# Second layer, second product of the last two batches: seven block products for eight, kept apart over the groups of weights

## The chip, the cores and the metric

The kernel runs on one core of a Trainium2 chip. The metric is the time of one execution in device microseconds, as a median over runs. In the profiles the engines are PE (TensorE), DVE (VectorE), ACT (ScalarE), POOL (GpSimd) and SP, on whose queue every DMA of this kernel is issued.

## The reference

Attention over four batches of 448 tokens, then two layers over 1792 tokens with a model width of 768 and an inner width of 2048. Only the last layer is touched:

```python
def _moe2_ref(x, w_in, w_out) -> np.ndarray:
    h = x @ w_in
    r = np.maximum(h, 0.0)
    g = r * r
    return (g @ w_out).astype(np.float32)
```

All data are float32. The kernel splits each float32 operand of a layer's products into an upper part in TensorE's own float32 form and a lower part (the rest), and sums three matmuls for each product: upper with upper, upper with lower, lower with upper.

## The kernel before, in words

`layer2` handles the four batches in two halves of two batches (896 tokens). In each half it goes through eight groups of weights; a group is two blocks of 128 inner features. For each group:

- **First product** (`seven`, line 1064). Four 448-token by 128-feature blocks of h come from seven block products instead of eight. Each is nine matmuls of 448 columns (line 1075). The sums of the products run on DVE (`plus`, line 1090: `g<-t`), and each finished block goes through `finish`: relu and square on ACT (lines 1338, 1344), then `split` into `gh` and `gl` (lines 523, 525: casts; line 532: subtraction, on DVE or POOL). In the trace the seven products are told by their operands: `pv<-raw,w` and `pv<-xb,w` are the two halves of p1, `t<-yb,w` are p6 and p7, `t<-xb,w` is p5, `t<-xb,v` is p4 and `t<-part,w` is p3.
- **Second product** (line 1367). Seven chunks of 128 tokens by two halves of 384 output columns, each the sum of six matmuls of 384 columns in a PSUM buffer `s`, of which there are four. That is 84 matmuls a group. One `acc` step per buffer adds it to the sum in SBUF, `gg` (line 1394, DVE; in the first group a copy on ACT, line 1388).
- After the last group each chunk of `gg` is stored (line 1408).

The weights of the first product are computed once, in the first half, and kept in DRAM as split parts (`sw`, `sz`, `sv`, `sa`); those of the second product too (`su`). In the second half all are loaded back (line 927) into a ring `w` of five buffers and `v`. The words of the second product's weights, not yet split, also lie in DRAM as `kq`.

Nothing fixes the order of the two layers by hand. Each operation is a `step` with the engines that may do it and their costs; a planner (`Plan.forward`, `Plan.backward`) takes the step that can start first by its own cost model, chooses between DVE, POOL and ACT, and issues everything in that order. A step that reads two SBUF tensors on DVE and any step on POOL exclude each other in the planner (the third entry of a cost). Attention has a written timetable, and isn't touched.

## Time and profile before

| | us |
|---|---|
| median of 3 runs | 1192.38 |
| the runs | 1186.67, 1192.38, 1195.06 |
| the profiled execution | 1184.83 |
| its span on the core | 1183.0 |

The profiled execution lies 7.55 us under the median, and 1.83 us of it are outside the span. All times of rows below belong to that one execution. A row of instructions gives their number, the mean duration of one, and the idle time of the engine just ahead of them with what ended it. Durations of DVE overlap where instructions follow each other without a gap: the busy time of a run of several tells how far their starts lie apart.

### The profile page before, as it was taken

The page shows a single profiled execution, that of the slowest core. Times are in us where ns is not written, and L with a number is a line of the kernel's source. Part 1 is how long each engine was busy: PE and PEld are TensorE (multiplying, and loading weights), DVE is VectorE, ACT ScalarE, POOL GpSimd, SP SyncE. Part 2 cuts the span into 40 slices and gives each one's busy share as a digit, 9 for nine tenths or more (in the row PEclk, how much of TensorE's full clock was granted, in tenths as well). Part 3 has the DMA queues.
Part 4 walks back from the last instruction along what each step waited for, and adds up shares of the span by engine and source line. Part 5 has one row for each costly group of instructions (what it writes and reads, how often), then busy time and mean ns, then how long its engine had stood idle before and what let it go on. Part 6 is the DMA issues. An engine that isn't in the chain of part 4 may idle for free.

```text
span 1183.0 us, 18930 instructions
## 1 busy us (share of the span) xinstructions
PE 1156.8 (98%) x6888; PEld 1035.5 (88%) x6888; DVE 921.4 (78%) x1612; ACT 551.3 (47%) x1154; POOL 239.4 (20%) x445
## 2 busy tenths in 40 slices
PE   5999999999999999999999999999999999999998
PEld 3777777778899999999999999899999989999997
DVE  7999999987999999965689898789887843555544
ACT  5999999874443334422325262544333423111111
POOL 3566676531000010000001020011131300000000
PEclk9999999999999999999999999999999999999999
DMA  7455557639998888732247649888768694444443
GB/s 171 86 78 90 90 91 102 96 63 204 298 285 271 251 276 289 228 110 63 82 172 228 240 153 359 268 298 310 262 245 293 191 322 154 147 147 147 149 170 122
DMA packets 136700, 224.86 MB, mean 190 GB/s; under 512 B 31392, under 2 KB 102048, under 8 KB 136608
## 3 DMA queue, kind: packets, MB, share of 16 engines
q1 hardware_dynamic: 136608, 223.67, 63.0%
q8 instruction: 54, 0.88, 0.4%
q14 instruction: 38, 0.31, 0.1%
HBM read 149.32 MB, written 74.31 MB: 189 GB/s over the span
## 4 chain that ended last, share of the span: by engine, by line
PE 91%; DVE 5%; DMA 3%; issue 1%; SPq 0%; ACT 0%; DVEq 0%; ACTq 0%
PE s L1164 19%; PE s L1367 18%; PE t L1075 18%; PE t L988 7%; PE t L712 7%; PE pv L1075 7%; PE pv L761 6%; PE s L685 6%; PE t L632 2%; DMA raw<-in_moe_w_in_dram 1%; DMA w<-sz 1%; DVE w L532 1%; DMA qk<-in_k_dram 0%; DVE g L1090 0%; DVE W L903 0%
## 5 line engine op out<-in xcount | busy, mean ns | idle before, releaser
L1164 PE MATMUL s<-gg,w 128*128 128x448 f32 x1152 | 238.8, 365 | 0.8 <-DVE gg L532 0.7
L1164 PEld LDWEIGHTS s<-gg,w 128*128 128x128 f32 x1152 | 216.2, 188 | 18.8 <-DVE gg L532 1.4
L1367 PE MATMUL s<-w,gh 128*128 128x384 f32 x896 | 227.7, 334 | 0.7 <-DVE gg L1394 0.7
L1367 PEld LDWEIGHTS s<-w,gh 128*128 128x128 f32 x896 | 162.3, 188 | 2.2 <-DVE gg L1394 1.1
L1090 DVE TENSOR_TENSOR g<-t,g 128x448 f32<-128x448 f32 x144 | 87.3, 620 | 93.1 <-ACT g L511 53.9
L1394 DVE TENSOR_TENSOR gg<-s,gg 128x384 f32<-128x384 f32 x196 | 107.0, 554 | 57.0 <-PE s L1367 56.6
L1367 PE MATMUL s<-w,gl 128*128 128x384 f32 x448 | 150.0, 335 | 0.9 <-DVE gl L532 0.8
L703 ACT ACTIVATE E<-s,mx 112x448 f32<-112x448 f32 x192 | 122.1, 647 | 20.6 <-ACT xf L511 13.0
L988 PE MATMUL t<-xb,w 128*128 128x448 f32 x576 | 119.2, 366 | 0.7 <-ACT g L1000 0.7
L988 PEld LDWEIGHTS t<-xb,w 128*128 128x128 f32 x576 | 108.0, 188 | 10.2 <-ACT g L1000 1.0
L523 ACT CAST w<-W 128x768 fp32r<-128x768 f32 (+1 forms) x73 | 54.5, 750 | 125.4 <-PE s L1164 46.5
L532 DVE TENSOR_TENSOR w<-W,w 128x768 fp32r<-128x768 f32 (+1 forms) x121 | 107.3, 896 | 6.8 <-ACT w L523 5.9
L696 DVE TENSOR_REDUCE mx<-s 112x1 f32<-112x448 f32 x192 | 107.4, 610 | 6.1 <-PE s L685 5.4
L712 PEld LDWEIGHTS t<-ident,E 112*112 112x112 f32 x768 | 73.8, 134 | 32.0 <-issue 14.6
L712 PE MATMUL t<-ident,E 112*112 112x112 f32 x768 | 95.3, 267 | 0.8 <-DVE T L648 0.4
L1367 PEld LDWEIGHTS s<-w,gl 128*128 128x128 f32 x448 | 84.1, 188 | 1.9 <-DVE gl L532 1.9
L761 PE MATMUL pv<-PT,vv 112*64 112x224 f32 x768 | 83.1, 359 | 0.0
L1075 PE MATMUL t<-yb,w 128*128 128x448 f32 x360 | 80.2, 372 | 2.4 <-DMA w<-sz 2.4
L1075 PE MATMUL t<-xb,w 128*128 128x448 f32 x360 | 79.9, 367 | 0.0
L511 ACT COPY g<-pv 128x448 f32<-128x448 f32 x24 | 12.7, 531 | 140.1 <-PE pv L1075 130.6
L1075 PEld LDWEIGHTS t<-yb,w 128*128 128x128 f32 x360 | 68.5, 191 | 8.5 <-DMA w<-sz 2.7
L685 PE MATMUL s<-T 64*112 64x448 f32 x576 | 73.1, 384 | 2.6 <-ACT T L641 1.9
(119 smaller groups left out, 1803.7 us busy)
## 6 DMA issues: line engine op xcount, KB each, us to landing
raw<-in_moe_w_in_dram SPq DMA_DIRECT2D x25, 768.0 KB
raw<-in_moe_w_out_dram SPq DMA_DIRECT2D x24, 512.0 KB
su<-w SPq DMA_DIRECT2D x16, 768.0 KB
w<-su SPq DMA_DIRECT2D x16, 768.0 KB
xf<-y SPq DMA_DIRECT2D x48, 224.0 KB
raw<-in_moe_w_out_dram SPq DMA_DIRECT2D x10, 768.0 KB
ki<-W SPq DMA_DIRECT2D x16, 384.0 KB
ko<-W SPq DMA_DIRECT2D x24, 256.0 KB
```

The costliest lines, as they stand in the source:

```text
L532: kind, when, any_t(n, rate), lambda e: engine(e).tensor_tensor(o(), a(), h(), ALU.subtract),
L685: nc.tensor.matmul(pts[j].ap[:CP, :S], T.ap[r, 0, a, c * CP:(c + 1) * CP], T.ap[r, 1, b_], start=(k_ == 0), stop=(k_ == 2),)
L696: lambda e, pt=pt, mx=mx: nc.vector.tensor_reduce(mx.ap, pt.ap[:CP, :S], AX.X, ALU.max, negate=True),
L703: lambda e, j=j, c=c, pt=pt, mx=mx, E=E: nc.scalar.activation(E.ap[:, j], pt.ap[:CP, :S], AF.Exp, bias=mx.ap, accum_out=sums.ap[:, j, c:c ...
L712: nc.tensor.transpose(pe.ap[:CP, m * CP:(m + 1) * CP], E.ap[:, j, m * CP:(m + 1) * CP], ident.ap)
L761: nc.tensor.matmul(pv.ap[j * D:(j + 1) * D, c2 * CT * CP:(c2 + 1) * CT * CP], vr.ap[:, j * NCH + m, :], pt.ap[:, j * NCH + m].rearrange("p ...
L988: nc.tensor.matmul(pt.ap[:, :S], w_()[:, c, :], x[c // HC].ap[:, a, c % HC, :], start=(c == 0 and n == 0), stop=(c == NC6 - 1 and n == 2),)
L1075: nc.tensor.matmul(pt.ap[:, :S], w_()[:, c0 + c, :], view(b, a, c)(), start=(start and c == 0 and k == 0), stop=(c == HC - 1 and k == 2), ...
L1090: lambda e: nc.vector.tensor_tensor(o.ap, pt.ap[:, :S], a.ap, ALU.add),
L1164: nc.tensor.matmul(pt.ap[:, :S], w_()[:, f, :], gg.ap[:, k, a, f, :], start=(f == 0 and n == 0), stop=(f == HQ - 1 and n == 2),)
L1367: nc.tensor.matmul(pt.ap[:, :NH], g.ap[:, fi, tc_ * P:(tc_ + 1) * P], w_()[:, 0, nh * NH:(nh + 1) * NH], start=(n == 0), stop=(n == 5),)
L1394: lambda e, o=o, pt=pt: nc.vector.tensor_tensor(o(), pt.ap[:, :NH], o(), ALU.add),
```

## The change

For the second half alone (`SEVEN2 = (1,)`), and there for the first seven of the eight groups, the second product is made in blocks too. Of the 896 tokens, 384 of each batch are taken as the two token halves (`LEFT`, three chunks of 128 each, `NPAIR`); the remaining 128 tokens (64 of each batch) are one chunk that is done as before. The two blocks of inner features and the two halves of 384 output columns are the other halves. The seven products of a group are added over the groups without being joined: P3, P4, P5 and C11 into the four places of `gg`, U2 and P7 into six buffers of the ring `xf`. Before the last group, which is done as before, `join` forms the result with five additions for each of the three chunks.

What is added for each of the seven groups:

- two loads of 384 KB (`V<-kq`), four differences of 384 columns (`w_sum`) and two splits of 768 columns (`w_hi2`, `w_lo2`) for the weights;
- four sums of 384 columns (`h_sum`) and four splits (into `part` and a buffer of the ring `W`) for g; one of the plain splits shrinks from 448 to 64 columns;
- 23 additions to SBUF in place of 14.

In these groups `seven` makes p5 ahead of p4 (`fifth`). In the last group the order of the chunks alternates between the batches, and the stores name their rows accordingly.

```diff
+SEVEN2 = (1,)
-    def seven(x, w, at, finish):
+    def seven(x, w, at, finish, fifth=False):
...
+        if fifth:
+            p5 = psum("t")
+            product(p5, z, 0, "T1")
+            plus(c21, u3, p5)
+            finish(1, 1, c21)
+            plus(u2, u2, p5)
+            c21 = u3
         p4 = psum("t")
         product(p4, a22, 0, "T4")
...
+            later = products7(total, LEFT, NPAIR) if half in SEVEN2 else None
             for fg in range(NG):
+                sums = later is not None and fg < NG - 1
...
+                    c0 = LEFT if sums and (fi, bi) == (1, 0) else 0
...
+                    if sums:
+                        later.sums(fi, bi, whole, at)
+                seven(x, w, ("end", t), finish, sums)
+                if sums:
+                    later.weights(f0, f1, at)
+                    t = later.down(gh, gl, wo, fg, t, DOWN2)
+                    continue
+                if later is not None:
+                    later.join(("end", t - 7 * PROD))
...
+    class products7:
+        def __init__(self, total, left, npair):
+            self.part = sb([P, 2 * NC6 * S // 2], FR, "part", None, "yp")
+            self.block = sb([P, 2 * HC * S], FR, "xb")
+            self.word = [sb([P, UW], FR, "W") for _ in range(2)]
+            self.more = {(n, m): sb([P, S], F32, "xf") for m in range(npair) for n in ("U2", "P7")}
...
+        def sums(self, fi, bi, g, at):
+            if (fi, bi) == (0, 0):
+                less(A22, A21, A22, ALU.add)
+                put("S1", A22)
+                less(A22, A22, A11)
+                put("S2", A22)
+                less(A21, A11, A21)
+                put("S3", A21)
+            if (fi, bi) == (0, 1):
+                less(A12, A12, A22)
+                put("S4", A12)
+
+        def weights(self, f0, f1, at):
+            W0, W1 = (second_out(f, at, "V", "yp") for f in (f0, f1))
+            less(W1, 0, W1, 1, W1, 0)
+            less(W1, 1, W0, 1, W1, 1)
+            less(W0, 1, W0, 1, W1, 0)
+            less(W0, 0, W0, 0, W0, 1)
+            for n, W in (("13", W1), ("42", W0)):
+                (h, hk), (l, lk) = self.T[n]
+                split(("w_hi2", "w_lo2"), at, h, l, lambda W=W: W.ap, [W], [hk, lk], DM)
+
+        def down(self, gh, gl, wo, fg, t, DOWN2):
+            ops = {
+                1: (raw(1, 1), given(1, 0)), 2: (raw(0, 1), given(0, 0)), 3: (summed("S4"), given(0, 1)),
+                4: (raw(0, 0), made("42", 0)), 5: (summed("S1"), made("13", 0)), 6: (summed("S2"), made("42", 1)),
+                7: (summed("S3"), made("13", 1)),
+            }
+            for n in (4, 5, 7, 1, 6, 3):
+                for m in range(self.npair):
+                    pt = psum("s")
+                    product(n, m, pt, True, t)
+                    add_to(*into({1: "U2", 6: "U2"}.get(n, f"P{n}"), m), pt, fg == 0 and n != 6, ("end", t))
+                    if n == 1:
+                        product(2, m, pt, False, t)
+                        add_to(*into("C11", m), pt, fg == 0, ("end", t))
...
+        def join(self, at):
+            for m in range(self.npair):
+                for n, a in (("P3", "U2"), ("P3", "P5"), ("U2", "P7"), ("P5", "U2"), ("P4", "U2")):
```

Here `product` issues three matmuls of 384 columns, `raw` are `gh` and `gl`, `given` the loaded weights, `summed` the four sums of g and `made` the differences of the weights. The line of the new matmuls is 1544, that of the plain ones 1422, of the additions 1438; other lines of the parts above move by one.

How the planner lays the work out has changed as follows. **TensorE, a late group of the second half** (from the middle of its first product on). Before:

```order
L1075 MATMUL t<-yb,w 128x448 x18
L1075 MATMUL pv<-raw,w 128x448 x9
L1075 MATMUL t<-xb,v 128x448 x9
L1075 MATMUL pv<-xb,w 128x448 x9
L1075 MATMUL t<-xb,w 128x448 x9
L1075 MATMUL t<-part,w 128x448 x9
L1367 MATMUL s<-w,gh 128x384 x2
L1367 MATMUL s<-w,gl 128x384
```

Now, rows that repeat a triple left out:

```order
L1076 MATMUL t<-xb,w 128x448 x9
L1076 MATMUL pv<-xb,w 128x448 x9
L1076 MATMUL t<-xb,v 128x448 x9
L1076 MATMUL t<-part,w 128x448 x9
L1544 MATMUL s<-xb,gh 128x384
L1544 MATMUL s<-W,gh 128x384
L1544 MATMUL s<-xb,gl 128x384
...
L1076 MATMUL pv<-raw,w 128x448 x9
L1544 MATMUL s<-xb,part 128x384 x18
L1544 MATMUL s<-w,gh 128x384 x2
L1544 MATMUL s<-w,gl 128x384
```

The 84 plain matmuls in one piece have become 63 new ones and 12 plain ones, and p1 of the next group (`pv<-raw`) has moved up to stand 9 matmuls after p3; products 5 and 7 (`s<-xb,part`) stand behind it.

**VectorE, the same group.** Before, where the second product is summed:

```order
L1090 TENSOR_TENSOR g<-t,g 128x448 x3
L525 CAST gh<-g 128x448
L1394 TENSOR_TENSOR gg<-s,gg 128x384 x2
L532 TENSOR_TENSOR gl<-g,gh 128x448
L1394 TENSOR_TENSOR gg<-s,gg 128x384 x12
```

Now:

```order
L1438 TENSOR_TENSOR gg<-s,gg 128x384 x3
L533 TENSOR_TENSOR part<-g,part 128x384
L1091 TENSOR_TENSOR g<-t,g 128x448
L1438 TENSOR_TENSOR gg<-s,gg 128x384 x3
L1438 TENSOR_TENSOR xf<-s,xf 128x384 x7
L1438 TENSOR_TENSOR gg<-s,gg 128x384 x2
L533 TENSOR_TENSOR W<-g,part 128x384
L1438 TENSOR_TENSOR gg<-s,gg 128x384
L1438 TENSOR_TENSOR xf<-s,xf 128x384 x2
L533 TENSOR_TENSOR W<-V,xb 128x768
```

Between the additions there now stand subtractions for the split parts (`W<-g,part`, `W<-V,xb`), and 15 additions answer to one stretch of 45 matmuls.

**TensorE, the end of the first half**, where the second half's p1 and p6 begin among the last 84 plain matmuls. Before:

```order
L1075 MATMUL pv<-raw,w 128x448 x9
L1367 MATMUL s<-w,gh 128x384 x2
L1367 MATMUL s<-w,gl 128x384
L1367 MATMUL s<-w,gh 128x384 x2
L1367 MATMUL s<-w,gl 128x384
L1075 MATMUL t<-yb,w 128x448 x9
```

Now:

```order
L1076 MATMUL pv<-raw,w 128x448 x9
L1422 MATMUL s<-w,gh 128x384 x2
L1422 MATMUL s<-w,gl 128x384
...
L1422 MATMUL s<-w,gh 128x384 x2
L1422 MATMUL s<-w,gl 128x384
L1076 MATMUL t<-yb,w 128x448 x9
```

There are 24 plain matmuls between the two now (6 before).

## Rows read from the trace of the kernel before

**Rows 1.** First part of the page: busy time, share, number of instructions by engine.

```profile
PE 1156.8 (98%) x6888; PEld 1035.5 (88%) x6888; DVE 921.4 (78%) x1612; ACT 551.3 (47%) x1154; POOL 239.4 (20%) x445
```

**Rows 2.** All waits of TensorE: total us, times, longest.

```profile
PE t L632 <- POOL y L611: 11.4, 1, 11.4
PE t L1075 <- DMA w<-sz: 2.4, 1, 2.4
...
PE s L1367 <- DVE gg L1394: 0.7, 1, 0.7
```

**Rows 3.** Chain that ended last, in order of time: start, us, what.

```profile
1108.52 14.56 PE s L1367 x84
1123.08 3.71 PE t L1075 x18
...
1136.06 14.56 PE s L1367 x84
```

**Rows 4.** Stretches: busy time of each engine, granted clock, DMA share, GB/s.

```profile
460.00:500.00 40.00, 40.00 (x199) 37.09 (x198) 37.43 (x68) 19.16 (x36) 2.58 (x2) 1.00 0.71 229
680.00:720.00 40.00, 40.00 (x199) 37.03 (x198) 37.77 (x66) 23.12 (x41) 7.32 (x5) 1.00 0.61 193
937.05:970.66 33.61, 30.03 (x149) 27.42 (x148) 16.39 (x31) 8.50 (x16) 7.06 (x6) 0.95 0.91 309
950.75:953.00 2.25, 2.25 (x6) 2.04 (x7) 0.00 (x0) 0.00 (x0) 0.00 (x0) 0.50 1.02 399
1073.00:1073.50 0.50, 0.50 (x4) 0.46 (x3) 0.00 (x0) 0.00 (x0) 0.00 (x0) 1.00 0.04 12
1108.36:1135.90 27.54, 27.54 (x149) 26.39 (x148) 14.20 (x26) 5.47 (x11) 1.16 (x1) 1.00 0.47 158
```

**Rows 5.** Instructions by line, whole span: count, busy us, mean ns, idle before.

```profile
L1394 DVE TENSOR_TENSOR gg<-s,gg 128x384 f32<-128x384 f32 x196 | 107.0, 554 | 57.0 <-PE s L1367 56.6
L1090 DVE TENSOR_TENSOR g<-t,g 128x448 f32<-128x448 f32 x144 | 87.3, 620 | 93.1 <-ACT g L511 53.9 <-PE t L1075 35.9 <-issue 1.3
L897 DVE SCALAR_TENSOR_TENSOR V<-raw,V 128x768 int32<-128x768 int32 x19 | 18.1, 952 | 0.3
L1052 DVE TENSOR_TENSOR W<-W 128x384 f32<-128x384 f32 x26 | 15.1, 592 | 0.3
L525 DVE CAST gh<-g 128x448 fp32r<-128x448 f32 x35 | 14.1, 409 | 15.2 <-ACT g L1344 15.1
L1052 POOL TENSOR_TENSOR W<-W 128x384 f32<-128x384 f32 x6 | 7.2, 1197 | 37.4 <-DVE W L1033 33.7 <-DVE w L532 3.7
L532 POOL TENSOR_TENSOR w<-W,w 128x768 fp32r<-128x768 f32 (+1 forms) x7 | 11.9, 1707 | 56.9 <-ACT w L523 56.9
```

**Rows 6.** Timeline between the halves, of all engines: start, us, what [idle before].

```profile
930.74 5.37 POOL L1216 TENSOR_TENSOR xf<-xf 128x448 f32<-128x448 f32 x1 [14.11 <-DMA xf<-y]
938.92 0.64 SPq L927 DMA_DIRECT2D w<-sz  x1
940.60 1.15 POOL L532 TENSOR_TENSOR xb<-xf,xb 128x448 fp32r<-128x448 f32 x1 [0.68 <-ACT xb L523]
941.03 0.97 DVE L525 CAST gh<-g 128x448 fp32r<-128x448 f32 x1 [2.34 <-ACT g L1344]
941.92 1.47 DVE L1394 TENSOR_TENSOR gg<-s,gg 128x384 f32<-128x384 f32 x3
942.52 0.62 PE L1367 MATMUL s<-w,gh 128*128 128x384 f32 x2 [0.75 <-DVE gg L1394]
945.18 2.10 PE L1075 MATMUL pv<-raw,w 128*128 128x448 f32 x9 [0.31 <-DMA w<-sw]
950.75 3.50 PE L1075 MATMUL t<-yb,w 128*128 128x448 f32 x9 [2.41 <-DMA w<-sz]
```

**Rows 7.** Timeline of SP in a late group: start, us, DMA issued.

```profile
1067.51 0.84 SPq L927 DMA_DIRECT2D w<-su  x2
1077.29 0.32 SPq L927 DMA_DIRECT2D w<-sw  x1
```

More of the change, by code (lines that the diff above doesn't have):

```diff
@@ L1107, in seven @@
         finish(0, 0, c11, p1)
-        p5 = psum("t")
-        product(p5, z, 0, "T1")
-        plus(u3, u3, p5)
-        finish(1, 1, u3)
-        plus(u2, u2, p5)
+        if not fifth:
+            p5 = psum("t")
+            product(p5, z, 0, "T1")
+            plus(u3, u3, p5)
+            finish(1, 1, u3)
+            plus(u2, u2, p5)
         p3 = psum("t")
@@ L1331, in layer2, with finish @@
                 gl = sb([P, 2, 2 * S], FR, "gl", 1, "yp")
-                def finish(fi, bi, g, src=None, gh=gh, gl=gl):
-                    k = slice(bi * S, (bi + 1) * S)
+                whole = {}
+                def finish(fi, bi, g, src=None, gh=gh, gl=gl, at=at, sums=sums, whole=whole):
                     step(
@@ L1359, in layer2 @@
+                chunks = [tc_ * P for tc_ in range(TC)]
+                if later is not None:
+                    chunks = [(1 - m % 2) * (2 * S - LEFT) + m // 2 * P for m in range(2 * NPAIR)] + [LEFT]
+                for tc_, c0 in enumerate(chunks):
                     for nh in range(2):
                         pt = psum("s")
-                        def products(e, gh=gh, gl=gl, wo=wo, tc_=tc_, pt=pt, nh=nh):
-                            n = 0
-                            for fi in range(2):
-                                _, _, wh, wl = wo[fi]
-                                for w_, g in ((wh, gh), (wl, gh), (wh, gl)):
-                                    nc.tensor.matmul(
-                                        pt.ap[:, :NH],
-                                        g.ap[:, fi, tc_ * P:(tc_ + 1) * P],
-                                        w_()[:, 0, nh * NH:(nh + 1) * NH],
-                                        start=(n == 0),
-                                        stop=(n == 5),
-                                    )
-                                    n += 1
@@ L1376, in layer2 @@
                         step(
-                            "down2", ("end", t), pe_t(DOWN2 / 2), products,
+                            "down2", ("end", t), pe_t(DOWN2 / 2),
+                            plain(gh, gl, wo, c0, pt, nh),
                             reads=[z for w in wo for z in w[:2]]
-                            + [(z, (fi, bi)) for z in (gh, gl) for fi in range(2) for bi in bs],
+                            + [(z, (fi, bi)) for z in (gh, gl) for fi in range(2)
+                               for bi in range(c0 // S, (c0 + P - 1) // S + 1)],
@@ L1380, in layer2 @@
                             writes=[pt],
                         )
[L1383 to L1396 removed]
+                        accumulate(total, tc_, nh, pt, fg == 0, t)
@@ L1413, in layer2, with plain, products @@
                             r0 = r1
+    def plain(gh, gl, wo, c0, pt, nh):
+        def products(e):
+            n = 0
+            for fi in range(2):
+                _, _, wh, wl = wo[fi]
+                for w_, g in ((wh, gh), (wl, gh), (wh, gl)):
+                    nc.tensor.matmul(
+                        pt.ap[:, :NH], g.ap[:, fi, c0:c0 + P], w_()[:, 0, nh * NH:(nh + 1) * NH],
+                        start=(n == 0), stop=(n == 5),
+                    )
+                    n += 1
+        return products
@@ new lines, in accumulate, with add_to @@
+    def accumulate(total, tc_, nh, pt, first, t):
+        add_to(lambda: total.ap[:, tc_, nh * NH:(nh + 1) * NH], (total, (tc_, nh)), pt, first, ("end", t))
+    def add_to(o, k, pt, first, at):
+        if first:
+            step("acc", at, act_t(NH), lambda e: nc.scalar.copy(o(), pt.ap[:, :NH]), reads=[pt], writes=[k])
+        else:
+            step(
+                "acc", at, dve_t(NH), lambda e: nc.vector.tensor_tensor(o(), pt.ap[:, :NH], o(), ALU.add),
+                reads=[pt], writes=[k],
+            )
```

126 lines of the change are left out of this document (101 added, 25 removed).

## The prediction, written before the changed kernel had run

> **What bounds the kernel now.** The page comes first: TensorE (PE) is busy for 1156.8 of 1183.0 us, 98% [rows 1]. Its waits come second. The largest, 11.4 us, is in the start-up; behind it only one is over 1 us, 2.4 us on a weight load, `w<-sz` [rows 2]. So from the start of the layers on, matmuls taken away are time taken away, as long as nothing else becomes late. Third, the chain of waits in the stretch that the change touches: in the second half of the second layer it never leaves PE. One group starts at 1108.52, the next at 1136.06; the 84 matmuls of its second product take 14.56 us, and the other 63 the rest of the 27.54 us [rows 3]. In that group PE is busy for 27.54 of 27.54 us, VectorE (DVE) for 14.20, ScalarE (ACT) for 5.47, GpSimd (POOL) for 1.16 [rows 4]. The side engines have room; the change spends it. Last, the one weak place: from 937.05 to 970.66, where the second half begins, PE does one group's work (84 matmuls of the second product, 63 of the first) in 33.61 us [rows 4] instead of 27.54, so 6.07 us are lost there.
>
> **The matmuls removed.** 14.56 us for 84 is 173.3 ns each [rows 3]. A group of before has 84 in its second product; one of the change has 7 x 3 x 3 = 63 in the block products and 12 in the plain chunk, so 9 fewer. Seven groups: 63 x 173.3 ns = **10.9 us less**. A changed group should take 27.54 - 1.56 = 25.98 us. The Trainium skill ("TensorE: Matmul & The Clock Gate", "Back-to-back issue gap") puts the spacing of matmuls at the full clock at columns / 2.4 + 2.5 ns, which is 162.5 ns for 384 columns and would make this term 10.2 us as an estimate; the row is longer, and the row is used.
>
> **DVE in a changed group.** From the order I count 44 instructions: 23 additions out of PSUM at 554 ns, 6 sums of the first product at 620, 9 two-input operations of 384 columns at 592, 2 of 448 (taken like the 620), 1 of 768 at 952, and 3 casts or small ones at no more than 409 [rows 5]. In full durations that is 12.7 + 3.7 + 5.3 + 1.2 + 1.0 + 1.2 = 25.2 us, 97% of 25.98. But the durations overlap: three additions in a row take 1.47 us together [rows 6], so their starts are 0.46 us apart, about 0.1 us less than a duration. With that, 44 instructions need 21.0 us, 81%. So DVE is between 81% and 97% full. Is that enough? Twice in the trace DVE is as full as that for 40 us, 37.43 and 37.77 us busy, and PE is busy for all 40.00 [rows 4]. I take it as hidden, with small waits: one of at most 0.75 us [rows 6] shows what a late addition costs. **I add 2.0 us** (seven groups at 0.3); the ends are 0 and, from the stretch below, 14.4.
>
> **ACT and POOL.** ACT gets, per group, at most six more casts or copies than the 11 instructions in its 5.47 us [rows 4]; even at 1 us each it stays under half of 25.98. POOL gets four more, three of 384 columns at 1.20 and one of 768 at 1.71 [rows 5], on top of its 1.16: 6.5 us. Both are hidden by the matmuls; what POOL does to DVE is a rival below.
>
> **The order of PE.** p1 of the next group now stands 9 matmuls behind p3, and its weights `w<-sw` go into the buffer that the second half of p1 has just freed. From there to its use lie p4, p3 and 9 matmuls: 1.86 + 1.86 + 1.56 = 5.28 us, where before it had the whole second product. Two such loads issued at 1067.51 [rows 7] had moved by 1073.0, since the DMA share is down to 0.04 in the half microsecond after [rows 4]: 5.5 us for both, so one needs less than that, about 3.5 us if half of the time beyond the start is its own. The cover remains, with 1 to 2 us to spare, and I cost it at nothing; if it were gone, it would be a wait on that load in every group. The wait on SP for that buffer has the load of `sz` queued behind it, which is needed only by p6, far later. Moving p5 ahead of p4 costs nothing either: the same nine matmuls.
>
> **DMA.** Two more loads of 384 KB in 25.98 us add about 30 GB/s to 158 GB/s at a share of 0.47 [rows 4]. There is room. The loads of the second group stand among the stores of the first half's result on SP, and are needed a whole group later.
>
> **Where the halves meet.** PE lost 6.07 us there. A good part is one event: p6 waited 2.41 us for `sz` and then took 3.50 us [rows 6] where two such products take 3.71 [rows 3], so 1.64 us more. In that stretch the granted clock was 0.50, the lower level of 1.2 GHz [rows 4], right after PE had stood still. The load was issued at 938.92 and p6 was reached 1.0 us of plain matmuls after p1. In the new order 24 plain matmuls stand between p1 and p6 instead of 6: 18 x 173.3 ns = 3.1 us more work, more than the 2.41 us of wait. If the load lands when it did, the wait goes, and the slow product with it: 4.05 us at most. The wait of p1 for `sw` (0.31, behind one of 0.75 for an addition) stays or grows, since that load isn't earlier. New there are the sums of g and of the weights of the first group, on a DVE that is full up to then. **I take 3.5 us off**; ends: 6.07 off, and 2.4 on, a second wait as large as the one there.
>
> **What I cost at nothing.** The join is 15 additions in the last group, on DVE and POOL: at 592 ns each [rows 5] under 9 us on top of 14.20, hidden by that group's 27.54. The tail behind the last matmul doesn't change: one addition and the stores. Attention keeps its written timetable. The planner has also reordered the first layer and the first half, as a whole; no wait there is longer than 0.8 us before, so there is little to win, and I allow 2 us either way for it.
>
> **The sum.** -10.9 - 3.5 + 2.0 = -12.4 us. From the profiled execution's 1184.83 that gives 1172.4. That execution was 7.55 us under the median of the runs, with the same work in it; against the median of 1192.38 it is **1180**.
>
> **The rivals.**
>
> *The four PSUM buffers become the wait.* In the stretch of 45 matmuls, 7.80 us, DVE has 15 additions, one subtraction of 384 and one of 768 columns. At 0.46 us of spacing it is done in about 8.2 us, and three buffers of lead (1.56 us) absorb the difference. At full durations it needs 8.3 + 0.6 + 1.0 = 9.9 us, 2.05 too much. Then PE waits for `s` in each group, up to 7 x 2.05 = 14.4 us, all of the gain. With 1.2 us a group it would be 1192.4 - 14.4 + 8.4 = **1186**. For it speaks that additions used to come every 1.04 us, two thirds idle around them, and now every 0.52; against it the overlap in the row. Chance 0.17.
>
> *Nothing is won where the halves meet*, since the loads and sums of the first group are as late as `sz` was. Then -10.9 + 2.0 gives **1183.5**. The first group has more to prepare on a full DVE; against it stand the 3.1 us of cover. Chance 0.18.
>
> *POOL shuts DVE out* (slower). Between the halves a cast that takes 409 ns [rows 5] took 0.97 us while POOL was in a subtraction of 1.15 us that had begun 0.43 us earlier, and the addition behind it was what PE then waited for, 0.75 us; a POOL operation of 448 columns took 5.37 us in a stretch where DVE had no gap [rows 6]. If each of the 6.5 us of POOL in a changed group stops DVE, DVE needs 21.0 + 6.5 = 27.5 up to 25.2 + 6.5 = 31.7 us, against 25.98. At the upper end PE loses 5.7 us in each of the groups that follow one another, six times: 34 us, and the time is 1192.4 - 14.4 + 34 = **1212**. It decides for slower than before from 2.1 us a group. Against it: most of DVE's instructions there are additions out of PSUM with one input in SBUF, and the planner keeps two-input operations of both engines apart. The Trainium skill ("SBUF — State Buffer", "Who interferes with whom") states this as a lock on a port that DVE and POOL share, which a DVE operation takes with two SBUF inputs, or in a copy or cast in a 2-port mode, and one with a single SBUF input doesn't; the cast of 0.97 us agrees. By that rule the 23 additions and the 6 sums would go on beside POOL, and only about 8 us of DVE's 21 would compete. Chance 0.10.
>
> **How the numbers follow.** The forecast, 1180, has 0.55. One per cent of the median, 11.9 us, is about what a measurement of this kernel can tell from no change; the forecast of 12.4 lies just beyond it, and its own ends (17.0 off with no new waits, to about 8 off) lie on both sides. So faster by over 1% is most of the forecast's chance, 0.50 with a little from the others; within 1% holds the rest of it and the two middle rivals, 0.41; slower by over 1% is the third rival's, 0.09. The range: 17.0 off is 1175, and since the three runs before spread over 8.4 us, a median can come out 4 us to either side: 1171 below. Above, it takes in the two middle rivals with that spread: 1190.
>
> **What would show it.** Right: groups of 26.0 us in the chain of the second half, on PE alone; DVE busy for 21 to 25 us in each, PE for all of it; 63 fewer matmuls; no wait of p6 for `sz`, and no stretch of half clock near 950. Wrong: waits of PE for `gg` or `xf` (the PSUM rival), for split parts in `part`, `W` or `xb` with POOL durations well over 1.2 us or casts near 1 us (the third rival), or for `w<-sw` in every group (the cover of p1). A group longer than 27.54 us would mean that the side engines set the pace.

## The result, and the profile after

The changed kernel takes **1176.37 us** (median of 14 runs, 1173.49 to 1183.66). The kernel before, run again beside it, takes 1184.51 us (median of 14 runs, the three shown earlier among them). The ratio is 0.9914 with a 95% interval of 0.9887 to 0.9942: 8.1 us faster, 0.9%. The prediction was 1180 with a range of 1171 to 1190. It subtracted 12.4 us from 1192.38, the median of the first three runs, which lies 7.9 us above the median of the fourteen. So the total came out 3.6 us from the forecast partly because two errors cancel, and the step to judge is the difference: 12.4 us forecast, 8.1 measured. The profiled execution after took 1178.22 us with a span of 1176.4, 6.6 us less than the one before.

The first part of the page after, which answers to [rows 1]:

```profile
PE 1148.1 (98%) x6825; PEld 1024.0 (87%) x6825; DVE 992.0 (84%) x1761; ACT 576.7 (49%) x1199; POOL 266.8 (23%) x469
```

There are 63 matmuls fewer, as announced; DVE has 149 instructions more. TensorE's waits (total us, times, longest), which answer to [rows 2]:

```profile
PE t L633 <- POOL y L612: 11.7, 1, 11.7
PE t L713 <- DVE PT L514: 1.8, 2, 1.5
PE s L1422 <- DVE gl L533: 1.7, 2, 0.9
...
PE s L1544 <- DVE part L533: 1.5, 4, 0.4
...
PE s L1422 <- DVE gh L526: 1.1, 1, 1.1
...
PE s L1544 <- ACT gg L1435: 0.6, 1, 0.6
```

The wait for `w<-sz` is gone, and none for an addition out of PSUM (`gg` or `xf` from line 1438) has come in the second half; one of 0.6 us is for a copy out of PSUM by ACT, in the first group. New are waits for `part`: the split sums of g, which the block products read.

The chain after, in order of time (start, us, what), which answers to [rows 3], and the same groups by engine in the windows view (start:end, us, then PE, PEld, DVE, ACT, POOL busy, granted clock, DMA share, GB/s), which answer to [rows 4]:

```profile
1065.34 2.08 PE s L1422 x12
1067.42 3.71 PE t L1076 x18
...
1091.36 2.08 PE s L1422 x12
1093.44 3.71 PE t L1076 x18
```

```profile
1067.42:1093.44 26.02, 26.02 (x140) 24.86 (x139) 22.18 (x44) 9.52 (x17) 6.02 (x5) 1.00 0.55 198
1093.44:1119.46 26.02, 26.02 (x140) 24.86 (x139) 22.17 (x44) 9.51 (x17) 6.03 (x5) 1.00 0.46 167
```

One group starts at 1067.42, the next at 1093.44: 26.02 us, against 25.98 forecast. PE is busy for all of it, DVE for 22.18 us, POOL for 6.02. These are two of the late groups, though. The starts of p3 (`t<-part,w`) in the timeline, from group to group, tell of all of them: 27.80, 27.36, 26.76, 26.48, 26.02, 26.01 and 24.93 us (before: 27.54 each). The first four are longer than a group's work by 1.8, 1.4, 0.8 and 0.5 us. The seventh stretch has 1.86 us less work, since half of the last group's p1 (`pv<-xb`) stands behind its p3: 24.16 is its work, and 0.8 us are lost there too.

Where is that time lost? These rows of TensorE's timeline after (start, us, what) show, in three groups, the `s<-xb,part` matmuls of products 5 and 7 with the row ahead of them, and in the last two the row behind them.

```profile
997.35 0.34 PE L1544 MATMUL s<-xb,gl 128*128 128x384 f32 x1
997.52 2.70 PE L1544 MATMUL s<-xb,part 128*128 128x384 f32 x11
1000.48 1.51 PE L1544 MATMUL s<-xb,part 128*128 128x384 f32 x7 [0.25 <-DVE part L533]
...
1051.64 2.00 PE L1076 MATMUL pv<-raw,w 128*128 128x448 f32 x9
1053.48 3.56 PE L1544 MATMUL s<-xb,part 128*128 128x384 f32 x18
1056.88 0.51 PE L1544 MATMUL s<-w,gh 128*128 128x384 f32 x2
...
1078.12 2.00 PE L1076 MATMUL pv<-raw,w 128*128 128x448 f32 x9
1079.96 3.30 PE L1544 MATMUL s<-xb,part 128*128 128x384 f32 x18
1083.10 0.51 PE L1544 MATMUL s<-w,gh 128*128 128x384 f32 x2
```

In the late group the 18 matmuls go from 1079.96 to 1083.10, 3.14 us or 174 ns each. One group earlier they take 3.40. In the group that starts at 994.10 the first 11 alone take 2.96, where 11 x 173.3 ns is 1.91: 1.05 us lost, of which the view of waits shows 0.25. The rest lies in starts that are late by too little to be printed as waits, or to show as idle time at all: a matmul's row lasts 0.33 us and the next starts 0.17 us after it. So the list of waits understates such losses; the spacing of the groups doesn't.

The three groups aren't laid out alike. In the late one p1 (`pv<-raw`) stands between the nine plain triples behind p3 and products 5 and 7, as the order of a late group had it. In the first two groups it doesn't. Products 5 and 7 follow the triples at once: in the second group 3.42 us after the start of p3 (994.10 to 997.52), in the late one 5.26 (1074.70 to 1079.96). The first sum of g starts as early in both, 2.07 and 2.08 us after p3:

```profile
996.17 0.56 DVE L1476 TENSOR_TENSOR g<-g 128x384 f32<-128x384 f32 x1 [0.72 <-ACT g L1359]
...
1076.78 0.56 DVE L1476 TENSOR_TENSOR g<-g 128x384 f32<-128x384 f32 x1 [0.72 <-ACT g L1359]
```

In the third group p1 is in its place, and PE waits 0.45 us for a subtraction that DVE makes beside one of POOL:

```profile
1024.68 1.21 POOL L1476 TENSOR_TENSOR g<-g 128x384 f32<-128x384 f32 x1 [7.53 <-DVE g L1476]
1024.93 1.48 DVE L1438 TENSOR_TENSOR gg<-s,gg 128x384 f32<-128x384 f32 x3
1026.04 1.16 POOL L533 TENSOR_TENSOR gl<-g,gh 128x448 fp32r<-128x448 f32 x1 [0.15 <-ACT gh L524]
1026.32 1.76 DVE L533 TENSOR_TENSOR part<-g,part 128x384 fp32r<-128x384 f32 x2
1027.67 1.51 PE L1544 MATMUL s<-xb,part 128*128 128x384 f32 x7 [0.45 <-DVE part L533]
```

The two subtractions take 1.76 us together, since the first alone takes 1.29: it begins 0.28 us after POOL's and ends 0.42 us after it. The seventh group repeats it, with 1.28 us and a wait of 0.44. Everywhere else in the second half this subtraction takes 0.54 to 0.55 us, but for one of 0.71 in the fourth group, also beside POOL.

Where the halves meet, which answers to [rows 6], in the timeline after:

```profile
942.88 2.56 POOL L533 TENSOR_TENSOR xb<-V,xb 128x768 fp32r<-128x768 f32 x1
945.78 2.00 PE L1076 MATMUL pv<-raw,w 128*128 128x448 f32 x9
948.90 0.44 PE L1422 MATMUL s<-w,gl 128*128 128x384 f32 x1 [0.78 <-DVE gl L533]
952.84 2.02 PE L1076 MATMUL t<-yb,w 128*128 128x448 f32 x9
```

p1 waits for nothing, and p6 at 952.84 takes 2.02 us where it took 3.50 behind a wait of 2.41. One wait of 0.78 for an operand of the plain matmuls is left.

To compare kernels, I cut each profiled span by TensorE's timeline into five stretches: up to the first matmul of the layers (**attention**); to the end of the first half's last p3 (**middle**); from there to the start of the second half's first p3 (**meeting**); to the last matmul (**rest**); and the tail, 4.6 to 4.9 us in all of them.

| kernel | attention | middle | meeting | rest |
|---|---|---|---|---|
| before | 273.3 | 663.7 | 31.75 | 209.38 |
| the change | 276.8 | 662.8 | 26.77 | 205.48 |
| the change, second profile | 273.4 | 661.9 | 26.75 | 205.64 |
| the change, third profile | 274.3 | 665.8 | 26.74 | 205.38 |

The two last columns repeat to 0.3 us for the change. The two first vary by 3.4 and 3.9 us between executions of the same instructions, as much as the effects in question; so the steps below are read from the two last. Much of that variation is a wait with a stretch of the lower clock behind it (last section). The meeting gave 5.0 us against the one profile of the kernel before. The rest gave 3.9 where 63 x 173.3 ns = 10.92 was due: its work would be 198.46 us, and **7.0 us were lost again**.

### The profile page after: what moved, and what is told of

Same layout as the page of the kernel before. It is cut to its first block, busy times and chain, and to the rows that moved or that the text cites. A ratio compares the mean times of both kernels' runs of the same rounds, so it can differ in the third digit from the quotient of the medians.

```text
span 1176.4 us, 19157 instructions
## 1 busy us (share of the span) xinstructions
PE 1148.1 (98%) x6825; PEld 1024.0 (87%) x6825; DVE 992.0 (84%) x1761; ACT 576.7 (49%) x1199; POOL 266.8 (23%) x469
## 5 line engine op out<-in xcount | busy, mean ns | idle before, releaser
L1422 PE MATMUL s<-w,gh 128*128 128x384 f32 x560 | 142.4, 335 | 1.1 <-DVE gh L526 1.1
L1438 DVE TENSOR_TENSOR gg<-s,gg 128x384 f32<-128x384 f32 x196 | 103.6, 550 | 23.4 <-PE s L1422 22.9
L989 PEld LDWEIGHTS t<-xb,w 128*128 128x128 f32 x576 | 107.9, 188 | 11.7 <-ACT g L1001 1.9
L533 DVE TENSOR_TENSOR w<-W,w 128x768 fp32r<-128x768 f32 (+1 forms) x121 | 103.2, 859 | 5.8 <-ACT w L524 4.6
L1422 PEld LDWEIGHTS s<-w,gh 128*128 128x128 f32 x560 | 101.5, 188 | 2.4 <-DVE gh L526 1.5
L524 ACT CAST w<-W 128x768 fp32r<-128x768 f32 (+1 forms) x67 | 50.4, 752 | 94.3 <-PE s L1173 28.8
L1422 PE MATMUL s<-w,gl 128*128 128x384 f32 x280 | 94.0, 336 | 1.7 <-DVE gl L533 1.7
L1353 ACT ACTIVATE g<-g 128x448 f32<-128x448 f32 x48 | 27.7, 577 | 125.6 <-DVE g L1091 125.1
L1076 PEld LDWEIGHTS t<-xb,w 128*128 128x128 f32 x360 | 67.6, 188 | 6.0
```

What stands on the lines that cost most here:

```text
L533: kind, when, any_t(n, rate), lambda e: engine(e).tensor_tensor(o(), a(), h(), ALU.subtract),
L989: nc.tensor.matmul(pt.ap[:, :S], w_()[:, c, :], x[c // HC].ap[:, a, c % HC, :], start=(c == 0 and n == 0), stop=(c == NC6 - 1 and n == 2),)
L1076: nc.tensor.matmul(pt.ap[:, :S], w_()[:, c0 + c, :], view(b, a, c)(), start=(start and c == 0 and k == 0), stop=(c == HC - 1 and k == 2), ...
L1422: nc.tensor.matmul(pt.ap[:, :NH], g.ap[:, fi, c0:c0 + P], w_()[:, 0, nh * NH:(nh + 1) * NH], start=(n == 0), stop=(n == 5),)
L1438: "acc", at, dve_t(NH), lambda e: nc.vector.tensor_tensor(o(), pt.ap[:, :NH], o(), ALU.add),
```

## Experiments

My theory: the matmuls are worth what was forecast, and what was lost went to operands that DVE delivers late. Rivals: fewer matmuls are worth less than 173.3 ns each; a fuller DVE and POOL slow the whole stretch; the join in the last group. Each ratio is to runs of the kernel before made beside it, in three sets, whose medians are 1185.36, 1186.67 and 1185.39 us.

**The change once more, twice.** No edit.

> The changed kernel again, beside the next three on the same chip. By the theory that the new time is PE's work plus the waits seen in its trace, the stretch from the end of the first half's last p3 to the last matmul takes 232 us again (241.1 before), and the time is 8 to 10 us under before. By the rival that part of the change's effect lies in the reordered first layer, the stretch ahead of it differs by more than 2 us from before also in this profile.

> The changed kernel once more, on the chip of the three above. The second half takes 232.3 us as in its two profiles so far; the stretches ahead of it may differ by some us from profile to profile, though no instruction does.

1176.26 us, ratio 0.9926 (0.9905 to 0.9948), and 1176.17 us, ratio 0.9907 (0.9872 to 0.9941). The table above has their stretches: meeting and rest take 232.39 and 232.12 us together, as expected.

**The matmuls alone.** The kernel before, in its order, with 63 matmuls not issued:

```diff
+ skip = half == 1 and fg < NG - 1 and 2 * tc_ + nh < 9
...
+ if skip and n == 4:
+     n += 1
+     continue
```

> The kernel before, with 63 matmuls of 384 columns not issued: one of six in nine of the fourteen sums of each of the second half's first seven groups (that part of the product is left out of the result). All other instructions stand in the same order. By the theory that matmuls bound the second half, groups take 25.98 us instead of 27.54, the stretch from the first half's last p3 to the last matmul 230.2 us instead of 241.1, and the time falls by 10.9 us. By the rival that a matmul taken out of a sum is worth less than its 173 ns because weight loads or the additions set the pace, it falls by less than 8 us.

1173.51 us, ratio 0.99 (0.9879 to 0.9921). The chain of this kernel:

```profile
960.37 3.71 PE t L1075 x18
...
969.66 13.01 PE s L1372 x75
982.66 3.71 PE t L1075 x18
```

75 matmuls take 13.01 us, 173.5 ns each, and every group 25.98. The rest is 198.45 us, 10.93 less than before. So the price of the matmuls is right to the hundredth, and the rival on it is out.

This run also shows how far the meeting of the kernel before can be trusted. Its instructions there are the same, and p6 waits as long for `sz`:

```profile
950.96 2.10 PE L1075 MATMUL t<-yb,w 128*128 128x448 f32 x9 [2.40 <-DMA w<-sz]
```

But p6 takes 2.10 us instead of 3.50, the granted clock is 1.00, and the meeting takes 29.95 us instead of 31.75. Against that the change gains 3.2 us there and not 5.0.

**The join.** The change without the additions that put the block products together in the last group:

```diff
- "join", at, any_t(NH), lambda e, o=o, i=i: engine(e).tensor_tensor(o(), o(), i(), ALU.add),
+ "join", at, any_t(NH), lambda e: None,
```

> The changed kernel without the fifteen additions of the join (the result's blocks are left unjoined); everything else in the same order. By the theory that these additions on DVE make the relu, square and split of the last group late, PE's wait of 1.1 us for gh ahead of the last 84 matmuls goes, with 0.6 us of slower matmuls and smaller gaps around it, and the time is 1.5 to 2 us under the changed kernel. By the rival that the wait comes from the order of the chunks alone (p3 stands only one product ahead of them), it stays over 0.8 us.

1175.71 us, ratio 0.9921 (0.9898 to 0.9943). Meeting and rest together are 231.63, 0.5 to 0.8 us less than in the three profiles of the change. Ahead of the last 84 matmuls one wait shrinks from 1.08 to 0.51 us. The join costs 0.5 to 0.8 us, less than the 1.5 to 2 of the theory; the rival, by which the wait stays over 0.8, is out as well.

**The preparation.** The change with the sums of g, the differences of the weights and their splits made in the first group only; the later groups read what it left:

```diff
- "h_sum", at, any_t(L), lambda e: engine(e).tensor_tensor(of(o), of(a), of(b), op),
+ "h_sum", at, any_t(L), lambda e: None if fg else engine(e).tensor_tensor(of(o), of(a), of(b), op),
...
+ if out:
+     step(kinds[0], when, copy_t(n), lambda e: None, reads=keys, writes=[writes[0]])
```

> The changed kernel with the sums of g, the differences of the weights and the splits of both made in the first group alone; later groups multiply those again (their own sums are left out of the result). Matmuls and additions are all there, in the same order. By the theory that the shortfall is late split parts, the waits for them in the second, third and seventh group (0.7 to 0.8 us each) go, those of the first group (1.7 us in all) stay, and the time is 2 to 2.5 us under the changed kernel. By the rival that the side engines' load slows PE throughout, all groups become shorter than 26.02 us, and the gain is over 4 us.

1173.65 us, ratio 0.9911 (0.9884 to 0.9938). The rest is 201.79, 3.7 us less than the change. Its stretch of 26 us among the late groups, by engine:

```profile
1066.00:1092.00 26.00, 26.00 (x140) 24.84 (x139) 17.32 (x34) 6.38 (x13) 1.16 (x1) 1.00 0.55 200
```

DVE is down to 17.32 us and POOL to 1.16, and the late groups take the same 26.02. The groups behind the first take 25.98 and 26.02 at once instead of 27.36, 26.76, 26.48. The order of the matmuls is that of the change. So the 22 us of DVE in a late group don't slow PE as such: 3.7 us, more than the 2 to 2.5 of the theory, hang on the preparation. The first group, which still prepares, keeps 27.50, and the wait ahead of the last 84 stays (1.02).

**Only the weights' preparation once.** As above, but the sums and splits of g stay:

```diff
- lambda e: engine(e).tensor_tensor(view(o, ko), view(a, ka), view(b, kb), ALU.subtract),
+ lambda e: None if fg else engine(e).tensor_tensor(view(o, ko), view(a, ka), view(b, kb), ALU.subtract),
```

> The changed kernel with the differences of the weights and their splits made in the first group alone, while g is summed and split in every group (the weights' part is left out of the result after the first group); all other instructions are in the same order. By the theory that the losses are the chain of g's sums and splits between p4 and product 7, with DVE's load deciding how late it gets, part of the 3.8 us that came back when nothing was prepared comes back: 1 to 2.5 us. By the rival that the weights' preparation, 768 columns at a time, is what holds DVE up, nearly all of it does, 3 us or more.

1175.51 us, ratio 0.9905 (0.9871 to 0.9939). The rest is 205.12, 0.3 us under the change: both theories had expected more. DVE has 19.12 us in a group, three less, and the waits for `part` stay, as TensorE's timeline shows:

```profile
1024.29 1.50 PE L1548 MATMUL s<-xb,part 128*128 128x384 f32 x7 [0.44 <-DVE part L533]
1129.43 1.51 PE L1548 MATMUL s<-xb,part 128*128 128x384 f32 x7 [0.44 <-DVE part L533]
```

These two runs together place the loss: of the 7.0 us, 3.7 hang on preparation, and by difference nearly all of that on the chain sum, cast, subtraction of g, which begins only when g of the group is there; a run without that chain alone wasn't made. Removing the weights' share of DVE, three us a group, gains next to nothing.

**p6 later, in the kernel before.** All 84 plain matmuls of the first half's last group stand ahead of p6:

```diff
- reads=[h, l] + [key(b, a, c) for a in range(2) for c in range(HC)], writes=[pt],
+ reads=[h, l] + [key(b, a, c) for a in range(2) for c in range(HC)], writes=[pt], after=after,
...
+ seven(x, w, ("end", t), finish, plain[:10] if half and fg == 0 else ())
```

> The kernel before, with one product moved: p6 of the second half's first group stands behind all 84 plain matmuls of the first half instead of 42 of them, so 48 plain ones between p1 and p6 instead of 6. Nothing is left out. By the theory that the changed order of these products is what won time where the halves meet, p6 no longer waits 2.4 us for its weights nor runs at the lower clock, and the stretch from the first half's last p3 to the next p3 falls from 31.75 us by 4 to 5 us, as it fell to 26.8 in the changed kernel; the time is 4 us under before. By the rival that the changed kernel won there by something else (fewer operand loads ahead of the weights), the stretch falls by less than 2 us.

1182.84 us, ratio 0.997 (0.9945 to 0.9995): 3.8 us. TensorE's timeline at the meeting:

```profile
946.59 2.10 PE L1075 MATMUL pv<-raw,w 128*128 128x448 f32 x9 [0.27 <-DMA w<-sw]
957.32 3.88 PE L1075 MATMUL t<-yb,w 128*128 128x448 f32 x18
```

The wait for `sz` and the slow p6 are gone, the meeting takes 28.29 us instead of 31.75, and the rest is 209.37, as before. This is the mechanism of the prediction alone, and it gives 3.5 us, a little under the 4 to 5 expected. Against the 29.95 us of the run without 63 matmuls, where p6 waited at the full clock, it would be 1.7.

**More load on DVE.** The change with eight more subtractions of 384 columns on DVE in each group, placed where the addition of the plain chunk must follow them:

```diff
+ EXTRA = 8
...
+ for _ in range(EXTRA):
+     step(
+         "more", ("end", t), dve_t(NH, 960.0, True),
+         lambda e: nc.vector.tensor_tensor(scratch(), scratch().bitcast(F32), scratch().bitcast(F32), ALU.subtract), writes=[(z, "z")],
+     )
...
- accumulate(total, 2 * self.npair, nh, pt, fg == 0, t)
+ accumulate(total, 2 * self.npair, nh, pt, fg == 0, t, [(z, "z")])
```

> The changed kernel with eight more subtractions of 384 columns on DVE in each of the seven groups (on a scratch area, each behind the one before; one addition of the group waits for them). By the theory that DVE has some 15% to spare in a group of 26.0 us, 3.7 us more fill it to 98 or 99%, groups grow by under 0.6 us and the time by under 4 us. By the rival that the additions on DVE already pace the stretch of 45 matmuls and any more work there shows in full, groups grow by 2 us or more and the time by over 12 us.

1180.61 us, ratio 0.9945 (0.9918 to 0.9973), 0.003 above the change's, or some 3.5 us. The rest is 209.57 us, 4.1 more; the meeting 29.29, 2.5 more. A stretch of 26 us among the late groups by engine, and waits of PE:

```profile
1066.00:1092.00 26.00, 25.21 (x130) 23.16 (x129) 25.02 (x46) 8.69 (x16) 8.93 (x8) 1.00 0.56 198
```

```profile
PE s L1545 <- DVE part L534: 2.4, 5, 0.8
PE pv L1077 <- DMA w<-sw: 1.8, 1, 1.8
...
PE s L1545 <- ACT part L525: 1.3, 1, 1.3
```

PE now stands still even in late groups, which take 27.50, 27.66 and 27.41 us, and again mostly for `part`; waits for additions out of PSUM come to 0.2. The result lies between the two expectations. It doesn't price DVE's time alone. The planner laid everything out anew: over the whole kernel DVE has only 24 instructions more than the change, POOL 25 and ACT 8, so that 33 others have left DVE. In those three groups DVE is busy for 25.95 to 26.29 us. The longest wait there, 0.62, is again for a subtraction beside one of POOL:

```profile
1082.57 1.01 POOL L534 TENSOR_TENSOR part<-g,part 128x384 fp32r<-128x384 f32 x1 [0.62 <-PE s L1545]
1082.63 1.37 DVE L534 TENSOR_TENSOR part<-g,part 128x384 fp32r<-128x384 f32 x1
```

And the 2.5 us at the meeting are no matter of the groups: p1 waits 1.8 for `sw`, and then takes 3.48 us at a granted clock of 0.55.

**Product 1 ahead of product 7.** The order of the block products in a group, so that `part` is needed later:

```diff
- for n in (4, 5, 7, 1, 6, 3):
+ for n in (4, 5, 1, 7, 6, 3):
```

> The changed kernel with products 1 and 2 ahead of product 7 in the list of a group's products, which fixes the order in which PSUM buffers are taken; the planner lays out everything anew. By the theory that the remaining loss is PE waiting for the split parts of the third sum of g in product 7, that sum gets 3.1 us more, the waits for part in the second, third and seventh group go, and the second half is 2 to 3 us shorter than the 232.3 us of the changed kernel. By the rival that product 2 then waits for its own block of g, which comes from p3, the last product, a wait for gh or gl stands in its place in most groups and the second half isn't shorter.

1177.06 us, ratio 0.9924 (0.9896 to 0.9951): no gain in the total. The rest is 205.06, 0.4 less than the change, and the meeting 25.72, 1.0 less: 1.5 together, where the theory had 2 to 3. The seventh group's wait is gone, but the group behind the second p3 now takes 28.31 us, and one of its waits is 0.70 for `part`. The late operands were only met elsewhere.

**The other batch first.** The order of the chunks in the second product of the last group, meant for the wait ahead of the last 84:

```diff
- for tc_, c0 in enumerate(chunks):
+ for tc_, c0 in (list(enumerate(chunks)) if later is None else [(n ^ 1, chunks[n ^ 1]) for n in range(2 * NPAIR)] + [(2 * NPAIR, LEFT)]):
```

> The changed kernel with the last group's chunks beginning with the other batch, whose blocks of g are made from p4 and p1 and not from p3; the planner lays out everything anew with that. By the theory that the wait of 1.1 us ahead of the last 84 matmuls is p3's chain through DVE and ACT, it falls under 0.5 us. By the rival that DVE, full with the join there, is late for any block, it stays over 0.8 us. The time is at most 1 us under the changed kernel, within what can be told.

1175.80 us, ratio 0.992 (0.9886 to 0.9954). The rest is 203.01, 2.5 us under the change, but not for the reason I gave: the wait ahead of the last 84 stays at 1.04, now for a cast on ACT. The theory fell. The middle takes 666.2 us, so the total doesn't differ from the change's.

About two thirds of what it won is in groups that the edit doesn't name. In the new layout no subtraction into `part` meets one of POOL, as the tile's instructions show (count, then ns as min/median/max; the change first):

```profile
L533 DVE TENSOR_TENSOR part<-g,part x17: 540/548/1291, 970.2 to 1135.1; 128x384 fp32r<-128x384 f32 x17
```

```profile
L533 DVE TENSOR_TENSOR part<-g,part x17: 547/551/557, 970.0 to 1133.0; 128x384 fp32r<-128x384 f32 x17
```

The third group takes 26.02 us instead of 26.76, and the waits of 0.45 and 0.44 are gone. The first two, where p1 still stands elsewhere, remain long: 27.12 and 27.29, where they were 27.80 and 27.36.

**Additions by ACT and POOL.** Product 7's additions as a copy on ACT and an addition on POOL, to relieve DVE:

```diff
+ if n == 7 and fg:
+     step("acc_copy", ("end", t), act_t(NH), lambda e, view=view, pt=pt: nc.scalar.copy(view(), pt.ap[:, :NH]),
...
+     step("acc_pool", ("end", t), pool_t(NH), lambda e, view=view, o=o: nc.gpsimd.tensor_tensor(o(), o(), view(), ALU.add),
```

> The changed kernel with the three additions of product 7 in the second to seventh group made in two steps, a copy out of PSUM by ACT and an addition in SBUF by POOL, in place of one addition on DVE; the planner lays out everything anew. Nothing is left out. By the theory that PE's remaining waits come from split parts queued on a full DVE, DVE is busy for about 21 us in a group instead of 22.2, the waits for part shrink, and the second half is 1 to 2 us shorter than 232.3 us. By the rival that POOL's additions, with two SBUF inputs, hold up DVE's two-input steps, it isn't shorter, and DVE's subtractions take over 0.7 us on the mean.

1185.51 us, ratio 0.9998 (0.9969 to 1.0027): the whole gain is gone. In the late group of 26.02 us DVE has 21.95, hardly less than 22.18, and the rest is 206.18, no better than the change. The second half isn't shorter, as the rival had it, but the subtractions into `part` stay under its 0.7 us with 639 ns on the mean; three of them take 0.80 to 1.23 us. The meeting is 29.45, with a wait of 1.89 and the lower clock behind it. Most was lost far from the edit. The planner had laid out the first half anew, and there TensorE's timeline shows:

```profile
744.62 3.64 PE L1076 MATMUL t<-part,w 128*128 128x448 f32 x9 [3.55 <-DVE g L1091]
```

and the windows view of that stretch:

```profile
744.62:748.10 3.48, 3.48 (x10) 3.12 (x10) 3.39 (x7) 2.24 (x5) 0.00 (x0) 0.51 1.01 421
```

PE waits 3.55 us, and then p3 takes 3.64 us instead of 2.0 at a granted clock of 0.51, the lower level: 5.2 us of the 6.3 by which the middle is longer than the change's.

**Three changes at once.** The two edits above, and the first group's copies out of PSUM on ACT or DVE:

```diff
- step("acc", at, act_t(NH), lambda e: nc.scalar.copy(o(), pt.ap[:, :NH]), reads=[pt], writes=[k])
+ both = {**act_t(NH), **dve_t(NH)} if at[1] > 200.0 else act_t(NH)
...
```

> The changed kernel with that change, with the last group's chunks beginning with the other batch, and with the copies of the first group on ACT or DVE as the planner chooses (all on ACT before). Nothing is left out. By the theory that the second half's losses are the first group's (1.8 us), the split parts' and the last group's, it takes 228 to 230 us instead of 232.3, and the time is 2 to 4 us under the changed kernel's. By the rival that each new layout loses elsewhere what it wins here, it is within 1 us of it.

1186.43 us, ratio 0.999 (0.9959 to 1.002). The middle is 667.8 us, the rest 209.49, 4.0 more than the change; waits of 1.11 us for `part`, 1.09 and 0.95 for copies into `gg` stand in the first two groups, and behind the last of them the granted clock is 0.53. Worse than either theory had it. None of these versions that compute everything beats the change by more than its interval.

## Why the prediction came out as it did

- **The matmuls removed, -10.9.** Right: 10.93 in the run that took away nothing else, and late groups of 26.02 against 25.98 forecast. (The list of waits before has one more over 1 us than the prediction says, 1.9 in attention; nothing in the sum rests on it.)
- **Where the halves meet, -3.5.** Right in its mechanism. The size can't be told to better than 1.8 us: against the profile of before the later p6 alone gives 3.5 and the change 5.0, against the run without 63 matmuls, where the clock didn't fall, 1.7 and 3.2. The slow p6, 1.64 us of the forecast, wasn't there in that execution. The waits for the addition (0.75) and for `sw` (0.31) ahead of p1, which I left standing, are gone too, with 0.78 for `gl` in their place. The sums of the first group, which I named as new on DVE there, cost their time after it, in that group's own block products.
- **Small waits, +2.0.** This is the step that failed, by 5.0 us. "I take it as hidden, with small waits" put 0.3 us on each of seven groups; the runs show 7.0 in all, and not evenly. About 3.2 us lie in the first two groups, where products 5 and 7 follow p3 without p1 between them, so that `part` is needed 1.8 us sooner. Another 1.5 lie in the third and the seventh, where DVE's subtraction stands beside one of POOL, and 0.5 in the fourth. Two groups lose nothing. What remains is about 1.8 in the last group, 1.08 of it the wait ahead of the last 84. I had asked whether DVE has enough time in a group, and had read one late group's order as that of all seven. It has the time: the late groups show it, and taking away 4.9 us of its work changes nothing in them. The question that decides is when the last of a chain of small operations is done, in each group's own order, since `part` is needed a few matmuls after g is made. The two windows of 40 us in [rows 4], which reassured me, say how full DVE was, not how soon after it can be made an operand is read.
- **The join, at nothing.** It costs 0.5 to 0.8 us, inside those 1.8.
- **p1's load, DMA, ACT, POOL at nothing.** Right: no wait for `w<-sw` in any group, and in the two late groups a DMA share of 0.46 to 0.55, ACT 9.5 us of 26, POOL 6.02 where 6.5 was forecast. As load they cost nothing; what POOL does to DVE is in the rivals.
- **The reordered first layer and first half, 2 us either way.** -0.9 in the middle, but one program repeats it only to 3.9 us. This can't be settled from these profiles.
- **The rivals.** The PSUM buffers didn't become the wait, beyond 0.6 us in the first group. (In [rows 5] the additions have 57.0 us of idle time to 107.0 busy: they were idle for about a third, not two thirds.) Where the halves meet something was won. POOL shuts DVE out where they meet, but seldom: DVE's 22.18 us lie in the forecast's 21.0 to 25.2, and yet the two longest waits for `part` are of that kind, so this rival, at 0.10, holds about 1.5 us of the shortfall. The Trainium skill ("SBUF — State Buffer", "Who interferes with whom") states that a DVE operation with at most one input in SBUF goes on beside POOL and one with two contends with it, and the trace agrees on both: three additions out of PSUM take 1.48 us beside a sum on POOL (1024.68 to 1025.89), as they took 1.47 before, while the subtraction with two inputs in SBUF takes 1.29 us beside POOL and 0.55 alone. The planner keeps the two apart in its own times; in the trace they meet.

The sum with measured terms: -10.9 - 5.0 + 7.0 = -8.9, the two last columns of the table, or -7.1 with the meeting's 3.2; the medians say -8.1. The profiled span fell by only 6.6 because its attention took 3.4 us longer.

What stays open: no run moved p1 alone in the first two groups, or kept POOL alone away from DVE's subtractions; their shares are read from the traces, and for POOL from the run with the other batch first, which was laid out anew. A backlog of the first group that is worked off, which the falling losses suggest, doesn't explain the seventh group, which loses as much as the third and by the same pair of subtractions. In the first group ACT makes the copies out of PSUM (14.92 us busy, 9.57 in a late group), and one of its waits is for such a copy; how much of its 1.8 us that is stays open. Nor was it tried to hold the first half's layout fixed while DVE's order in the changed groups is altered, which the runs with the other batch first and with additions by ACT and POOL would have needed to show their own effect alone.

## What to carry to other kernels

When TensorE sets the pace, the spacing of its own rows priced removed matmuls exactly here; the uncertain term is the operands that must now be derived. Price those as a chain from the moment its input exists to the matmul that reads it, group by group, in each group's own order, and not by the busy share of the engine that derives them. Look at which operations of DVE and POOL will stand side by side. Where stretches upstream vary by more than the effect, compare stretch by stretch, and where a planner lays out the program anew, look at the stretches that the edit doesn't name: one wait there ate a whole gain.

## What the runs showed of the hardware

The list of waits has 1.5 us for `part`, in four waits, where the spacing of the groups shows a loss of over 4 us. The fourth group loses 0.5 us with PE busy for all of it:

```profile
1048.22:1074.70 26.48, 26.48 (x140) 24.78 (x139) 22.35 (x44) 9.05 (x18) 5.93 (x5) 1.00 0.56 193
```

A wait of PE can cost twice, but needn't. In the run with additions by ACT and POOL, p3 took 3.64 us right after PE had stood still for 3.55, against 2.02 elsewhere; the granted clock was 0.51 there, as it was 0.50 behind the wait for `sz` [rows 4, 6]. Both are the lower of the two levels, 1.2 GHz. Behind the same wait for `sz`, 2.40 us long, the run without 63 matmuls kept the full clock. The same pair explains much of what differs between executions of one program. In the first profile of the change PE waits 1.52 us for DVE in attention, at 233.88, and then has the lower clock; in its third profile it waits 2.67 us at 294.02, in the middle, where the second waits 1.35 and keeps the full clock:

```profile
235.00:238.40 3.40, 3.40 (x21) 2.70 (x18) 2.60 (x6) 2.77 (x8) 2.41 (x11) 0.50 0.70 41
```

```profile
295.50:298.80 3.30, 3.30 (x10) 2.94 (x10) 3.23 (x6) 1.00 (x2) 0.00 (x0) 0.50 1.07 369
```

For spacing of matmuls, the estimate of 162.5 ns comes from a formula that the Trainium skill ("TensorE: Matmul & The Clock Gate", "Back-to-back issue gap") gives for isolated matmuls. It stays under what is measured here, 173.5 ns in the run that removed the matmuls alone, where each has its own weights to load.

DVE and POOL also clash outside the changed groups. In attention, the first profile of the change (first two rows), and its second (last):

```profile
230.25 1.15 POOL L785 TENSOR_TENSOR xf<-xf,R 128x448 f32<-128x448 f32 x1 [2.93 <-DMA R<-rd]
230.40 1.02 DVE L733 TENSOR_SCALAR sum<-sum 112x8 f32<-112x8 f32 x1
```

```profile
228.81 0.16 DVE L733 TENSOR_SCALAR sum<-sum 112x8 f32<-112x8 f32 x1
```

The same operation takes 1.02 us beside a POOL operation and 0.16 alone. The wait of 1.52 us at 233.88 follows, and that execution ends attention 3.4 us later than the other. The sum also came 1.6 us later to begin with, so the clash is a part of this at most.
